# Attention and two MLP layers in one kernel: the first eight attention units in pairs, the second layer's raw weights fetched earlier, and operands of the sums split two ahead

## The chip, the cores and the metric

The kernel runs on one NeuronCore of a Trainium2 chip. Its time is device microseconds of one execution. TensorE (PE) multiplies matrices, VectorE (DVE) and ScalarE (ACT) work elementwise, and SyncE (SP) issues nearly all DMA. PE's weight loads have a track of their own (PEld).

## The reference

```python
# local and global attention: batch 4, 8 heads, 512 local + 32 global positions, head 64
s_g  = scale * q_g @ concat(k_g, k_l).T          # global rows see everything
out_g = softmax(s_g) @ concat(v_g, v_l)
s_ll = where(abs(pos_i - pos_j) <= 32, scale * q_l @ k_l.T, -1e9)
s_lg = scale * q_l @ k_g.T                       # local rows see a band and the global keys
out_l = softmax(concat(s_lg, s_ll)) @ concat(v_g, v_l)
x = concat(out_g, out_l)                         # 2176 tokens of 512
h = x @ w_in;  g = max(h, 0) + alpha * min(h, 0);  x = g @ w_out      # 512 -> 2048 -> 512
h = x @ w_in2; g = h * clip(h + 3, 0, 6) / 6;      out = g @ w_out2
```

All in float32 at full precision. The weights reach the chip as 64-bit words (float64).

## The kernel before, in words

Every product of the two layers is made of three: an operand is split into a rounded high part and the low rest, and high × high, low × high and high × low are summed. The high part is a copy on ACT, the low part a subtraction on DVE.

*Attention.* A unit is one batch, one half of the local positions and one pair of heads; there are 32. `local_units` (line 167) is a generator, and each `yield` ends a step. `load` fetches `q_t` and `k_t` (L173, L175), `load_v` the values `v_t` (L180). `scores` gives `s_ps` (L194); `softmax` reduces with the mask on DVE (L207), takes the exponential on ACT (L211) and the reciprocal `rs` on DVE; `transposes` makes `pt` (PE L222, copied by ACT L224); `values` gives `o_ps` (L235), scaled into `xo` by DVE (L241). The first eight units (`SINGLE`) run one at a time, the other 24 in pairs of two. `mask`, `ident` and `alpha` are loaded at the start (L73 to L75), `c1_sb` = 1 − alpha comes from the last of them (L76). `global_units` computes the 32 global rows of a pair of heads: `gq`, `gqz`, `gk`, `gv`, `gvg` are loaded (L302 to L310), scores `gs_ps`, transposes, and `go_ps` (L357): for each of the two heads four chunks of local values on 128 partitions and one of global values on 32.

*First layer.* `x_from_attention` transposes `xo` into `xt` (PE L386, ACT L372, DVE L373). A piece of weights is loaded as `raw` (L98) and turned into float32 on ACT (L113) and DVE (L117, L121, L123) as `z`, then split (ACT L129, DVE L130) into `wt`. There are five blocks of tokens (512, 512, 512, 256, 256). For each of 16 pieces j, `h_tile` gives `h_ps` (L401), `act` the activation `t`, `g` (ACT L411, DVE L413, ACT L419, DVE L420), and two steps later `y_tiles` adds into `y_ps` (L432). Block 0 runs as two lanes of 256 columns, the second four pieces behind; four products of zeros (L931) open its banks. The first layer's weights are converted during block 0. After each piece `attention_steps(STEPS[bi][s])` runs attention steps, and `SPLIT[bi]` steps of `second_weights` are spread over blocks 1 to 4: this generator fetches raws of the second layer, converts, splits, forms sums and differences, and stores them to DRAM (`wi` and `wo`, L506). Four buffers (`RAW`) are shared by raws and parts.

*Second layer.* It runs in two passes of 4 × 512 and 4 × 384 columns with seven products in place of eight. First the "in" products `k_ps` (L750) make tiles `far`; then the "sum" products `o_ps` (L830) take operands built from `far` by `operand` and split as `gh` (ACT L799) and `gl` (DVE L800). Weights stream from DRAM into eight buffers `ws` (L664 from `wi`, L669 from `wo`), issued by SP ahead of use. `inputs` prepares the input of the next pass meanwhile, one step per `next(more)`. The fifth block's rest follows (L897, L688).

The order of instructions on each engine is set by a scheduler when the program is built; what is wrapped in `here` keeps the order in which it is written. Each engine works its list in order, and an instruction waits for its inputs and for a free buffer (`bufs=`).

## Time and profile before

| | us |
|---|---|
| median of 3 runs | 855.52 (853.48 to 856.38) |
| the profiled execution | 853.92 |
| its span in the trace | 852.0 |
| PE busy | 827.0 (97%) |
| DVE busy | 592.8 (70%) |
| ACT busy | 415.2 (49%) |
| mean granted PE clock | 0.987 of full speed |

The span runs from the first to the last instruction; the execution's time is 1.9 us longer. A share of busy time is a mean over stages with different limits: attention with block 0 lies up to about 137 us, blocks 1 to 4 with the rest of attention and the second weights' preparation up to 497 us, and the second layer after it. The clock is given in shares of the full 2.4 GHz; the other level is 1.2 GHz.

### The profile page before, as it was taken

The page shows a single profiled execution, that of the slowest core. Times are in us where ns is not written, and L with a number is a line of the kernel's source. Part 1 is how long each engine was busy: PE and PEld are TensorE (multiplying, and loading weights), DVE is VectorE, ACT ScalarE, POOL GpSimd, SP SyncE. Part 2 cuts the span into 40 slices and gives each one's busy share as a digit, 9 for nine tenths or more (in the row PEclk, how much of TensorE's full clock was granted, in tenths as well). Part 3 has the DMA queues.
Part 4 walks back from the last instruction along what each step waited for, and adds up shares of the span by engine and source line. Part 5 has one row for each costly group of instructions (what it writes and reads, how often), then busy time and mean ns, then how long its engine had stood idle before and what let it go on. Part 6 is the DMA issues. An engine that isn't in the chain of part 4 may idle for free.

```text
span 852.0 us, 18369 instructions
## 1 busy us (share of the span) xinstructions
PE 827.0 (97%) x7232; PEld 745.6 (88%) x7232; DVE 592.8 (70%) x1321; ACT 415.2 (49%) x905; POOL 0.2 (0%) x4
## 2 busy tenths in 40 slices
PE   8898999999999999989999999999999998999997
PEld 5688999888878888878899998889999998999996
DVE  4898896576777777777778837879854787854221
ACT  5766665554556555455546523435532343443222
POOL 0000000000000000000000000000000000000000
PEclk7899999999999999999999999999999999999999
DMA  8994664476667765599776657668666887888882
GB/s 312 307 318 155 210 235 132 136 233 217 195 235 253 259 223 199 179 357 337 266 269 239 196 166 232 217 208 266 210 197 215 288 297 246 270 266 259 292 253 73
DMA packets 75780, 200.65 MB, mean 235 GB/s; under 512 B 7856, under 2 KB 24496, under 8 KB 74672
## 3 DMA queue, kind: packets, MB, share of 16 engines
q1 hardware_dynamic: 75600, 199.37, 70.4%
q8 instruction: 57, 0.93, 0.4%
q14 instruction: 27, 0.22, 0.1%
q10 hardware_dynamic: 96, 0.13, 0.1%
HBM read 157.00 MB, written 42.47 MB: 234 GB/s over the span
## 4 chain that ended last, share of the span: by engine, by line
PE 68%; DVE 12%; DMA 10%; ACT 7%; issue 2%; SPq 1%; ACTq 0%; DVEq 0%
PE o_ps L830 17%; PE k_ps L750 15%; PE y_ps L432 12%; PE h_ps L401 11%; DMA raw<-in_w 6%; PE h_ps L897 4%; PE o_ps L688 4%; DVE z L121 2%; DVE t L413 2%; ACT p L211 2%; PE s_ps L194 2%; DVE z L123 1%; ACT raw L113 1%; DMA ws<-wo 1%; DVE g L420 1%
## 5 line engine op out<-in xcount | busy, mean ns | idle before, releaser
L432 PE MATMUL y_ps<-g,wt 128*128 128x256 f32 (+2 forms) x1152 | 208.8, 332 | 5.8 <-ACT g L419 3.1
L401 PE MATMUL h_ps<-xt,wt 128*128 128x256 f32 (+2 forms) x1152 | 209.0, 331 | 1.8 <-ACT wt L129 0.8
L432 PEld LDWEIGHTS y_ps<-g,wt 128*128 128x128 f32 x1152 | 177.2, 191 | 23.1 <-ACT g L419 3.5
L401 PEld LDWEIGHTS h_ps<-xt,wt 128*128 128x128 f32 x1152 | 179.0, 191 | 20.5 <-DVE wt L130 1.5
L830 PE MATMUL o_ps<-ws,gh 128*128 128x256 f32 x784 | 141.1, 283 | 3.4 <-DMA ws<-wo 3.0
L750 PE MATMUL k_ps<-bt,ws 128*128 128x512 f32 (+1 forms) x672 | 136.8, 362 | 0.0
L750 PEld LDWEIGHTS k_ps<-bt,ws 128*128 128x128 f32 x672 | 120.8, 188 | 12.7
L830 PEld LDWEIGHTS o_ps<-ws,gh 128*128 128x128 f32 x784 | 121.2, 191 | 4.9 <-DMA ws<-wo 3.7
L830 PE MATMUL o_ps<-ws,gl 128*128 128x256 f32 x392 | 108.3, 283 | 0.0
L800 DVE TENSOR_TENSOR gl<-far,gh 128x1024 fp32r<-128x1024 f32 (+1 forms) x56 | 60.8, 1089 | 38.5 <-ACT gh L799 38.1
L799 ACT CAST gh<-far 128x1024 fp32r<-128x1024 f32 (+1 forms) x56 | 52.4, 942 | 63.3 <-PE o_ps L830 53.2
L830 PEld LDWEIGHTS o_ps<-ws,gl 128*128 128x128 f32 x392 | 73.6, 191 | 0.2
L413 DVE SCALAR_TENSOR_TENSOR t<-t,c_sb,h_ps 128x256 f32<-128x256 f32 (+2 forms) x96 | 55.2, 588 | 26.2 <-ACT t L411 26.0
L420 DVE TENSOR_TENSOR g<-t,g 128x512 fp32r<-128x512 f32 (+2 forms) x84 | 49.1, 586 | 23.1 <-ACT g L419 21.7
L419 ACT CAST g<-t 128x512 fp32r<-128x512 f32 (+2 forms) x84 | 45.0, 538 | 40.8 <-DVE t L413 36.4
L411 ACT ACTIVATE t<-h_ps 128x512 f32<-128x512 f32 (+2 forms) x84 | 42.8, 511 | 42.6 <-PE h_ps L401 39.3
L113 ACT ACTIVATE raw<-raw,quarter_sb 128x512 uint32<-128x512 uint32 x64 | 49.7, 777 | 26.4 <-DMA raw<-in_w 26.0
L211 ACT ACTIVATE p<-p,st 128x128 f32<-128x128 f32 x128 | 49.7, 390 | 16.6 <-DVE st L207 16.4
L735 ACT ACTIVATE t<-far,half_sb 128x512 f32<-128x512 f32 (+1 forms) x48 | 32.2, 670 | 47.4 <-DVE far L731 47.2
L121 DVE SCALAR_TENSOR_TENSOR z<-z,raw 128x512 uint32<-128x512 uint32 x64 | 43.9, 690 | 5.5 <-ACT raw L113 3.0
L123 DVE SCALAR_TENSOR_TENSOR z<-raw,z 128x512 uint32<-128x512 uint32 x64 | 43.7, 689 | 0.6
L897 PE MATMUL h_ps<-xt,ws 128*128 128x384 f32 x192 | 36.0, 336 | 0.0
(104 smaller groups left out, 868.5 us busy)
## 6 DMA issues: line engine op xcount, KB each, us to landing
ws<-wi SPq DMA_DIRECT2D x80, 512.0 KB, 4.9
ws<-wo SPq DMA_DIRECT2D x72, 512.0 KB, 4.3
raw<-in_w SPq DMA_DIRECT2D x64, 512.0 KB, 5.6
v_t<-in_vE SPq DMA_DIRECT2D x32, 512.0 KB, 6.6
wi<-raw SPq DMA_DIRECT2D x16, 512.0 KB, 2.9
wi<-parts SPq DMA_DIRECT2D x16, 512.0 KB, 4.6
wo<-raw SPq DMA_DIRECT2D x16, 512.0 KB, 3.2
wo<-parts SPq DMA_DIRECT2D x16, 512.0 KB, 6.1
```

The source lines that it names most:

```text
L113: here(nc.scalar.activation(low, low, AF.Relu, bias=quarter_sb, scale=0.9 * 2.0 ** -29))
L121: nc.vector.scalar_tensor_tensor(out=bits, in0=bits, scalar=3, in1=low, op0=ALU.logical_shift_left, op1=ALU.bitwise_or)
L211: nc.scalar.activation(p[:, n, :], p[:, n, :], AF.Exp, bias=st[:, 1, n:n + 1], scale=-1.0, accum_out=st[:, 2, n:n + 1])
L401: nc.tensor.matmul(ps[:, a:b], lhsT=wts[j][:, 0, wl, 128 * c:128 * c + 128], rhs=xt[c][:, xl, a:b], start=k == 0, stop=k == 3 * NC - 1)
L413: nc.vector.scalar_tensor_tensor(out=t[:, c:d], in0=t[:, c:d], scalar=c1_sb[:, j:j + 1], in1=ps[:, c:d], op0=ALU.mult, op1=ALU.add)
L420: nc.vector.tensor_tensor(out=g[:, 1, a:b], in0=t[:, a:b], in1=g[:, 0, a:b].bitcast(F32), op=ALU.subtract)
L432: nc.tensor.matmul(y[c][:, a:b], lhsT=wts[j][:, 1, wl, 128 * c:128 * c + 128], rhs=g[:, gl, a:b], start=first, stop=last)
L750: nc.tensor.matmul(bank, lhsT=wt[:, wl, at:at + 128], rhs=bt[x][:, c, xl, 0:w], start=first and k == 0, stop=k == 5, skip_group_check=True)
L799: nc.scalar.copy(hi, src)
L800: nc.vector.tensor_tensor(out=lo, in0=src, in1=hi.bitcast(F32), op=ALU.subtract)
L830: nc.tensor.matmul(bank, lhsT=part[:, jp, 128 * c:128 * c + 128], rhs=wo[:, jp, 256 * wl:256 * wl + 256], start=opens, stop=k == NP // 2 - ...
L897: nc.tensor.matmul(h, lhsT=wt[:, wl, 128 * c:128 * c + 128], rhs=xt[c][:, xl, 0:w], start=k == 0, stop=k == 3 * NC - 1)
```

## The change

- The first eight units run in pairs like the others. Scores of the first two pairs are computed before any transpose. SP loads the mask first, `ident` and `alpha` later, q and k of units 0 to 3 before any values; the values of these units go into free weight tiles, `vE` has two buffers instead of three. The early weight conversions come at other steps (`CONVERT`).
- `second_weights` fetches its next raw two steps earlier, and does none of its steps in the first two pieces of a block (`REST`).
- `global_units` multiplies the four local chunks of both heads first and then the global chunk of both.
- The four products of zeros that open the banks of block 0 are gone.
- In the stream, an "in" tile of which only one half is used is loaded by half.
- The operands of the sums come from a generator and are split two ahead, the first two during the last two rounds of the "in" products. One subtraction is done later (for "s3" instead of after "11"). The next pass's input preparation follows `MORE` and is kept in program order.

```diff
-SINGLE = 2 * HP
-SKEW = 1
-CONVERT = (5, 7, 9)
+CONVERT = (3, 4, 5)
+MORE = (1, 0, 8, 0, 0, 0, 8)
+REST = 2
...
     def load_constants():
-        nc.sync.dma_start(out=mask_sb, in_=mask)
         nc.sync.dma_start(out=ident_sb, in_=ident)
+        yield
         nc.sync.dma_start(out=alpha_sb, in_=alpha)
-        nc.vector.tensor_scalar(out=c1_sb, in0=alpha_sb, scalar1=-1.0, scalar2=1.0, op0=ALU.mult, op1=ALU.add)
+        yield
+        here(nc.vector.tensor_scalar(out=c1_sb, in0=alpha_sb, scalar1=-1.0, scalar2=1.0, op0=ALU.mult, op1=ALU.add))
...
         def load_v(u):
             b, hf, hp = units[u]
-            v_t[u] = att.tile([128, 8, 2, D], F32, tag="vE", name="v_t", bufs=3)
+            if u < FIRST_UNITS:
+                if u % 2 == 0:
+                    v2[u // 2] = wp.tile([128, 2, 8, 2, D], F32, tag="w", name="v_t", bufs=NJ)
+                v_t[u] = v2[u // 2][:, u % 2]
+            else:
+                v_t[u] = att.tile([128, 8, 2, D], F32, tag="vE", name="v_t", bufs=2)
...
         load(0)
-        load_constants()
+        nc.sync.dma_start(out=mask_sb, in_=mask)
         load(1)
+        constants = load_constants()
+        next(constants)
+        load(2)
+        load(3)
+        yield
         load_v(0)
-        load(2)
+        load_v(1)
+        next(constants)
         yield
-        load(3)
-        load_v(1)
+        pairs = [(u, u + 1) for u in range(0, n, 2)]
+        scores(*pairs[0])
         load_v(2)
+        load_v(3)
         yield
-        for lo, hi in ((0, FIRST_UNITS), (FIRST_UNITS, SINGLE)):
-            ...
-        pairs = [(u, u + 1) for u in range(SINGLE, n, 2)]
-        for j in range(len(pairs) + 1):
-            if j:
+        scores(*pairs[1])
+        next(constants, None)
+        load(4)
+        load(5)
+        yield
+        for u in pairs[0]:
+            transposes(u)
+        yield
+        values(*pairs[0])
+        load_v(4)
+        load_v(5)
+        for u in pairs[1]:
+            transposes(u)
+        yield
+        values(*pairs[1])
+        yield
+        for j in range(2, len(pairs) + 1):
+            if j > 2:
                 for u in pairs[j - 1]:
                     transposes(u)
                 yield
                 yield
             if j < len(pairs):
                 scores(*pairs[j])
-            if j:
+            if j > 2:
                 values(*pairs[j - 1])
             yield
             if j < len(pairs):
                 for u in pairs[j]:
-                    load_v(u)
+                    if j > 2:
+                        load_v(u)
                     if j + 1 < len(pairs):
                         load(u + 2)
             yield
...
+            os = [bank("go_ps") for _ in range(2)]
+            for cs in (range(4), range(4, 5)):
+                for h in range(2):
+                    pt, pt2 = pts[h]
+                    for c in cs:
+                        for b in range(B):
+                            nc.tensor.matmul(os[h][W * b:W * b + W, 0:D],
...
                 sums(z0, z1, k == 0)
                 store()
+                fetch()
                 yield
                 st = parts_tile()
                 hi(z, st)
                 yield
                 lo(z, st, dst[2 + k])
-                fetch()
                 yield
...
-            if key[0] == "in":
+            if key[0] == "in" and key[1] < len(twos) and key[3] == 1:
+                half = in_parts[key[2]][:, 1].rearrange("p (h c) -> p h c", h=2)[:, :, 256:512]
+                nc.sync.dma_start(out=t.bitcast(F32)[:, :, 256:512], in_=half)
+            elif key[0] == "in":
                 nc.sync.dma_start(out=flat, in_=in_parts[key[2]][:, key[3]])
...
+            def operands():
+                for what, _ in PRODUCTS:
+                    for pair in far:
+                        yield operand(what, pair)
+
+            coming, split = operands(), []
             for m in range(NP):
+                if m >= NP - 2:
+                    split.append(next(coming))
...
                 for k in range(NP // 2):
-                    hi, lo = operand(PRODUCTS[i][0], far[k])
+                    split.extend(islice(coming, 1))
+                    hi, lo = split.pop(0)
                     wo = take("sum", n, i, k)
...
-                    if i:
+                    for _ in range(MORE[i] * (k + 1) // (NP // 2) - MORE[i] * k // (NP // 2)):
                         next(more, None)
...
-            opened = still
-            for t in y:
-                nc.tensor.matmul(t, lhsT=still.to_broadcast([128, 128]), rhs=still.to_broadcast([128, 512]),
-                                 start=True, stop=False)
...
-            for _ in range(SPLIT[bi] * (s + 1) // (end + LAG) - SPLIT[bi] * s // (end + LAG)):
+            done = [SPLIT[bi] * max(x - REST, 0) // (end + LAG - REST) for x in (s, s + 1)]
+            for _ in range(done[1] - done[0]):
                 next(second, None)
```

How the program's order changes is seen at three places. The first is TensorE's list at the start, before and then after; `s_ps` are scores (sixteen rows to a unit), `pt_ps` transposes, `o_ps` values.

```order
L90 MATMUL warm_ps<-still 128x512 x8
L194 MATMUL s_ps<-k_t,q_t 32x128 x24
L222 MATMUL pt_ps<-ident_sb,p 128x128
L194 MATMUL s_ps<-k_t,q_t 32x128 x8
L222 MATMUL pt_ps<-ident_sb,p 128x128 x3
L194 MATMUL s_ps<-k_t,q_t 32x128 x8
```

```order
L92 MATMUL warm_ps<-still 128x512 x8
L201 MATMUL s_ps<-k_t,q_t 32x128 x64
L229 MATMUL pt_ps<-ident_sb,p 128x128 x9
L242 MATMUL o_ps<-v_t,pt 32x64 x16
L229 MATMUL pt_ps<-ident_sb,p 128x128 x5
L242 MATMUL o_ps<-v_t,pt 32x64 x16
```

The scores of four units now stand in one piece ahead of the first transpose; before, halves of units 1 and 2 stood between transposes.

The second is VectorE's list from the first `xo` on, before and then after; `z<-raw` begins a conversion of weights, `wt` ends it, `p,st<-s_ps` is a reduction of scores. Ahead of these rows stand twelve reductions before and sixteen after.

```order
L241 TENSOR_TENSOR xo<-o_ps,rs 128x256
L117 TENSOR_SCALAR z<-raw 128x512
L213 TENSOR_SCALAR st<-st 128x4
L215 RECIPROCAL rs<-st 128x4
L207 ISA p,st<-s_ps,mask_sb 128x128
...
L121 SCALAR_TENSOR_TENSOR z<-z,raw 128x512
L241 TENSOR_TENSOR xo<-o_ps,rs 128x256
L123 SCALAR_TENSOR_TENSOR z<-raw,z 128x512
```

```order
L248 TENSOR_TENSOR xo<-o_ps,rs 128x256 x2
L220 TENSOR_SCALAR st<-st 128x4
L222 RECIPROCAL rs<-st 128x4
L78 TENSOR_SCALAR c_sb<-alpha_sb 128x16
L119 TENSOR_SCALAR z<-raw 128x512 x2
L123 SCALAR_TENSOR_TENSOR z<-z,raw 128x512 x2
L388 TENSOR_TENSOR xt<-xt_ps,xt 128x256
L125 SCALAR_TENSOR_TENSOR z<-raw,z 128x512
```

The reductions of the fourth unit, which before stood inside the first conversion, have moved ahead of it, and the first two conversions run side by side.

The third is SP's list around the first global unit, before and then after; `raw<-in_w` are raw weights of the second layer here, `wo` its parts on the way to DRAM.

```order
L98 DMA raw<-in_w 128x512
L506 DMA wo<-parts 128x1024
L506 DMA wo<-raw 128x1024 x2
L302 DMA gq<-in_qgT 128x128
L304 DMA gqz<-in_qgT 64x128 x2
L306 DMA gk<-in_kN 128x2176
L308 DMA gv<-in_vN 128x2048
L310 DMA gvg<-in_vgN 32x512
L98 DMA raw<-in_w 128x512
```

```order
L100 DMA raw<-in_w 128x512
L521 DMA wo<-parts 128x1024
L100 DMA raw<-in_w 128x512
L521 DMA wo<-parts 128x1024
L521 DMA wo<-raw 128x1024
L314 DMA gq<-in_qgT 128x128
L316 DMA gqz<-in_qgT 64x128 x2
L318 DMA gk<-in_kN 128x2176
L320 DMA gv<-in_vN 128x2048
L322 DMA gvg<-in_vgN 32x512
L521 DMA wo<-raw 128x1024
L100 DMA raw<-in_w 128x512
```

Counted from the first raw of the second layer, the one straight behind `gvg` was the 53rd of 64. Now the 53rd is the second of the two ahead of `gq`, and the one behind `gvg` is the 54th.

## Rows read from the trace of the kernel before

**Rows 1.** The page's first part: busy us, share of the span, instructions.

```profile
PE 827.0 (97%) x7232; PEld 745.6 (88%) x7232; DVE 592.8 (70%) x1321; ACT 415.2 (49%) x905; POOL 0.2 (0%) x4
```

**Rows 2.** Stretches of the span: length, busy us by engine, PEclk, DMA share, GB/s.

```profile
0.00:16.00 16.00, 12.25 (x153) 7.76 (x159) 3.99 (x33) 7.41 (x28) 0.20 (x4) 0.74 0.85 283
16.00:34.00 18.00, 15.04 (x240) 11.51 (x239) 15.77 (x50) 12.46 (x35) 0.00 (x0) 0.76 1.00 341
34.00:137.00 103.00, 96.87 (x1206) 88.27 (x1196) 92.81 (x254) 69.48 (x172) 0.00 (x0) 1.00 0.66 224
...
360.00:380.00 20.00, 17.66 (x177) 15.58 (x176) 15.04 (x40) 10.50 (x26) 0.00 (x0) 0.91 1.01 354
...
560.00:600.00 40.00, 38.87 (x255) 35.19 (x254) 36.67 (x53) 20.58 (x33) 0.00 (x0) 1.00 0.80 258
```

**Rows 3.** Timeline of VectorE, 0 to 35 us: start, duration, what, [idle before it].

```profile
15.67 0.42 DVE L241 TENSOR_TENSOR xo<-o_ps,rs 128x256 f32<-128x256 f32 x1 [1.24 <-PE o_ps L235]
16.01 0.42 DVE L117 TENSOR_SCALAR z<-raw 128x512 f32<-128x512 f32 x1
...
17.14 0.29 DVE L207 CUSTOM_DVE_ANT_0 p<-s_ps,mask_sb 128x128 f32<-128x128 f32 x1 [0.41 <-PE s_ps L194]
...
17.99 0.69 DVE L121 SCALAR_TENSOR_TENSOR z<-z,raw 128x512 uint32<-128x512 uint32 x1
...
23.00 1.29 DVE L123 SCALAR_TENSOR_TENSOR z<-raw,z 128x512 uint32<-128x512 uint32 x2
...
33.77 0.87 DVE L413 SCALAR_TENSOR_TENSOR t<-t,c_sb,h_ps 128x256 f32<-128x256 f32 x2
```

**Rows 4.** Timeline of TensorE, 0 to 35 us.

```profile
8.02 1.08 PE L194 MATMUL s_ps<-k_t,q_t 64*32 64x128 f32 x16 [2.83 <-DMA k_t<-in_kE]
...
15.94 1.11 PE L194 MATMUL s_ps<-k_t,q_t 64*32 64x128 f32 x32
16.98 0.90 PE L222 MATMUL pt_ps<-ident_sb,p 128*128 128x128 f32 x3
```

**Rows 5.** Timeline of SP's DMA issues, 0 to 20 us.

```profile
3.06 0.43 SPq L173 DMA_DIRECT2D q_t<-in_qT  x1
3.53 0.43 SPq L175 DMA_DIRECT2D k_t<-in_kE  x1
```

**Rows 6.** Groups by line and shape on TensorE: busy us, mean ns.

```profile
L931 PE MATMUL y_ps<-still 128*128 128x512 f32 x4 | 2.2, 604 | 0.0
```

**Rows 7.** Timeline of all engines, 355 to 382 us.

```profile
359.25 0.63 SPq L98 DMA_DIRECT2D raw<-in_w  x1
...
368.09 0.43 DVE L117 TENSOR_SCALAR z<-raw 128x512 f32<-128x512 f32 x1 [1.79 <-DMA raw<-in_w]
...
371.60 0.41 ACT L419 CAST g<-t 128x256 fp32r<-128x256 f32 x1 [2.40 <-DVE z L123]
...
372.06 2.21 PE L432 MATMUL y_ps<-g,wt 128*128 128x256 f32 x12 [2.34 <-ACT g L419]
...
379.30 0.65 PE L357 MATMUL go_ps<-gv,gpt 128*32 128x64 f32 x32
...
379.89 0.31 PE L357 MATMUL go_ps<-gvg,gpt 32*32 32x64 f32 x8
```

**Rows 8.** The page's DMA issues: count, KB each, median us to landing.

```profile
ws<-wi SPq DMA_DIRECT2D x80, 512.0 KB, 4.9
ws<-wo SPq DMA_DIRECT2D x72, 512.0 KB, 4.3
raw<-in_w SPq DMA_DIRECT2D x64, 512.0 KB, 5.6
```

**Rows 9.** Waits by engine and line: us in total, times, longest.

```profile
PE o_ps L830 <- DMA ws<-wo: 3.0, 2, 2.3
...
PE o_ps L830 <- ACT gh L799: 0.5, 2, 0.3
...
DVE z L117 <- DMA raw<-in_w: 12.1, 9, 4.0
```

More of the change, by code (lines that the diff above doesn't have):

```diff
@@ L1 @@
 from contextlib import ExitStack
+from itertools import islice
 import numpy as np
@@ L168, in local_units @@
         units = [(b, hf, hp) for b in range(B) for hf in range(2) for hp in range(HP)]
-        q_t, k_t, v_t, p_t, rs_t, pt_t = {}, {}, {}, {}, {}, {}
+        q_t, k_t, v_t, p_t, rs_t, pt_t, v2 = {}, {}, {}, {}, {}, {}, {}
         def load(u):
@@ L200, in softmax @@
             b, hf, hp = units[u]
[L201 removed]
+            p = att.tile([128, 4, 128], F32, tag="p", name="p", bufs=FIRST_UNITS)
             st = att.tile([128, 4, 4], F32, tag="st", name="st", bufs=4)
@@ L421, in act, with y_tiles @@
         return g
-    def y_tiles(layer, y, g, wts, parts, opened=None):
+    def y_tiles(layer, y, g, wts, parts, lanes=False):
         for a, b, j in parts:
@@ L428, in y_tiles @@
             for (wl, gl), c in steps:
-                first = opened is None and j == 0 and (wl, gl) == (0, 0)
-                last = j == NJ - 1 and (wl, gl) == (0, 1) and (opened is None or b == 512)
+                first = a == 0 and j == 0 and (wl, gl) == (0, 0)
+                last = j == NJ - 1 and (wl, gl) == (0, 1) and (not lanes or b == 512)
                 if layer == 0:
                     nc.tensor.matmul(y[c][:, a:b], lhsT=wts[j][:, 1, wl, 128 * c:128 * c + 128], rhs=g[:, gl, a:b],
-                                     start=first, stop=last)
+                                     start=first, stop=last, skip_group_check=lanes)
                 else:
@@ L599, in columns, with inputs @@
         return sum(w for _, _, w in two[0])
-    def inputs(two, bt):
+    def inputs(two, bt, keep=lambda x: x):
         n = columns(two)
@@ L752, in product, with wide, total, parts_of @@
                         k += 1
+            def wide(tile_):
+                return tile_[:, :, 0:w]
+            def total(pool_):
+                return [pool_("o_ps") for _ in range((chunks + 1) // 2)]
+            def parts_of(src):
+                hi = wide(work.tile([128, 2, 512], F32R, tag="g", name="gh", bufs=LAG + 1))
+                lo = wide(later["xs"].tile([128, 2, 512], F32R, tag="gl", name="gl", bufs=3))
+                nc.scalar.copy(hi, src)
+                nc.vector.tensor_tensor(out=lo, in0=src, in1=hi.bitcast(F32), op=ALU.subtract)
+                return hi, lo
+            def operand(what, pair):
+                (a11, a12), (a21, a22) = ([pair[th][:, :, jh] for jh in range(2)] for th in range(2))
+                if what == "s1":
+                    add(a21, a21, a22)
+                elif what == "s2":
+                    add(a21, a21, a11, ALU.subtract)
+                elif what == "s4":
+                    add(a12, a12, a21, ALU.subtract)
+                elif what == "s3":
+                    add(a11, a22, a21, ALU.subtract)
+                return parts_of({"11": a11, "s1": a21, "12": a12, "s2": a21, "s4": a12, "s3": a11, "22": a22}[what])
+            def operands():
[3 more added lines that the diff above has]
+            coming, split = operands(), []
             for m in range(NP):
+                if m >= NP - 2:
+                    split.append(next(coming))
                 if m % 2 == 0:
@@ L787, in second_layer @@
             else:
[L788 to L819 removed]
+                more = inputs(twos[n + 1], bt_next, here)
             def summed(i, y, first=True):
                 for k in range(NP // 2):
[L823 removed]
+                    split.extend(islice(coming, 1))
+                    hi, lo = split.pop(0)
                     wo = take("sum", n, i, k)
```

73 lines of the change are left out of this document (11 added, 62 removed).

## The prediction

> **What bounds the kernel now.** I read the profile in this order: shares by engine, a table by stage, the list of waits, then the start and the 360–380 us stretch instruction by instruction. TensorE is busy 827.0 of 852.0 us [rows 1], so all that can be won without dropping matrix products is the 25.0 us in which it idles, and time in which it runs at the lower of its two clock levels, 1.2 instead of 2.4 GHz. The table by stage says where these lie [rows 2]: 3.75 us idle in 0–16, 2.96 in 16–34, 6.13 in 34–137, 2.34 in 360–380, 1.13 in 560–600 (stage length less PE's busy time), at mean clocks of 0.74, 0.76, 1.00, 0.91 and 1.00. The reader should see a second thing in the same rows: in 34–137 VectorE is busy 92.81 of 103 us. That stage, block 0, is paced by VectorE, which converts the first layer's weights there, and PE gets nothing to do before VectorE delivers. So the start matters through the time at which VectorE begins this work, not through PE's own idle time.
>
> The change touches five of these places. Each is priced against the profiled execution, 853.92 us; the median of the runs shown is 855.52, and I carry the sum over to it at the end.
>
> **1. The start.** VectorE's first weight conversion starts at 16.01, straight behind the first `xo` at 15.67, and the first `t` of the first layer, from which on block 0 runs, at 33.77 [rows 3]. Before that VectorE only reduces scores and waits for them. Scores of units 1 and 2 are computed in halves with transposes between; a half takes 1.08 us and can't start before unit 1's `k_t`, issued at 3.53, lands at 8.02, which is 4.49 us [rows 4, 5].
>
> After: SP issues mask, q1, k1 without ident and alpha between, two slots of 0.47 us earlier [rows 5], so k1 lands at 8.02 − 0.95 = 7.1, and k2, k3 (issued at 4.0 and 5.0 by the same slots, 4.5 us each) at 8.5 and 9.5. A whole unit's scores, undivided and at the low clock, took 1.11 us [rows 4]. So unit 1 is done at 8.2, unit 2 at 9.6, unit 3 at 10.6. Nine transposes stand next (three took 0.90 [rows 4], so 2.7: 13.3), then the values of unit 0 (1.1), five transposes (1.5), the values of unit 1 (1.1): 17.0, of which about half a microsecond overlaps, then two `xo` at 0.34 apart. The first conversion thus starts near 16.8, some 0.8 later than now. But all sixteen reductions of four units lie before it, where twelve do now. Between it and the first `t` the new order has four conversions of four operations, four `xt`, two `xo` and eight reductions. By [rows 3] these cost, less the 0.08 by which neighbours overlap (two of 0.69 take 1.29): 4 × (0.34 + 3 × 0.605) = 8.6, 4 × 0.335 = 1.3, 2 × 0.335 = 0.7, 8 × 0.215 = 1.7, together 12.3. First `t` at 16.8 + 12.3 = 29.1 instead of 33.77: 4.6 earlier. Before it, though, the old order had also done three of a fifth conversion's four operations (1.55) and the new one has done four reductions more (0.86), so 0.7 less work is behind it. **−3.9 us**, carried through block 0 because VectorE paces it. Bounds: if four units' scores run at the rate of the halves (2.1 us a unit), they end 3 us later and the gain is −1; if the clock stays high in the start and transposes and values take half, −6.5; and nothing, if raw weights or the loads ahead of them are late.
>
> The pairing itself, and the four opening products on zeros (604 ns each by the row, 2.2 us in all [rows 6]), lie where PE waits for VectorE. I count 0 for them; if that cover were gone, up to −2.2 for the zeros.
>
> **2. Fetch earlier, and the stall at 368.** SP issues the raw weights at 359.25, behind `gq`, `gk`, `gv`, `gvg`, over 2 MB; they land at 368.09, after 8.8 us, against a median of 5.6 [rows 7, 8]. VectorE's conversion waits 1.79 for them; its chain then holds the `t` behind which ScalarE's `g` starts at 371.60, and PE stands still 2.34 us until 372.06. The stage's mean clock of 0.91 over 17.66 busy us is another 1.6 us lost. In the new order on SP this raw, the 53rd of 64, goes out before `gq`. So the wait goes: 2.34 plus 1.0 of the 1.6 (a stretch at the low clock follows the stand): **−3.3 us**. Bounds: −3.9 and 0, the latter if `gk` then lands late and holds `gs` instead.
>
> The fetch also goes earlier in every other step of the split. That adds a wait on SP for a free raw buffer, and what is queued behind it there are loads of q, k, v and raws of the first layer. VectorE waits 12.1 us in all for raw weights, in nine places [rows 9]; the move may take some of these or add some. In 137–360 I see no PE idle time worth having, so 0 there.
>
> **3. Global units.** Per unit PE runs 32 products on 128 partitions (0.65 us) and 8 on 32 partitions (0.31), twice [rows 7]. Merged, one change of form is left of two. If the second group of eight costs what 8 of the 32 do (0.16), it saves 0.15 a unit: four units, **−0.5 us**. Bounds 0 and −1.2 (both groups).
>
> **4. The second layer.** PE waits 3.0 us in two places for the first `wo` weights of a pass and 0.5 for `gh` [rows 9]. Operands split two ahead take away the 0.5. Sixteen `in` loads are halved to 256 KB, so eight tiles' queue is shorter ahead of the first `wo`. That `wo` is issued only when a buffer comes free, though, and only some 12 products cover it, as now. I count 0.3 of the 3.0. **−0.8 us**; bounds −3.5 (both waits gone) and +3 (operand splits ahead of `far`, in program order, hold up the last `in` products: VectorE is 36.67 of 40 us busy in 560–600 [rows 2]). The moved subtraction is the same operation at another place: 0.
>
> The Trainium skill bears on the halved loads: its page "Perfetto Trace Analysis", section "DMA Optimizations", says "Small DMAs (< 2KB) have significant per-transfer overhead". The new pieces are 1 KB where they were 4 KB. In this trace the `wo` loads, in 2 KB pieces, take 4.3 us and the `wi` loads, in 4 KB pieces, 4.9 for the same 512 KB [rows 8], so no overhead shows down to 2 KB; no row here shows a 1 KB piece of this size. [...]
>
> **5. An allowance.** Queues, buffers (`vE` from three to two) and the order of the input split change in many places. One wait of the size of that in 560–600 (1.13) will come up somewhere: **+1.0 us**.
>
> Sum: −3.9 − 3.3 − 0.5 − 0.8 + 1.0 = −7.5, so 846.4 for a profiled execution, and 855.52 − 7.5 = **848.0** for the median, which I predict.
>
> **The rivals.**
> - *The start's gain is absorbed in block 0.* For it: VectorE waits for raw weights [rows 9], DMA is at 1.00 of its engines in 16–34 [rows 2], and values for four units are now loaded ahead of them. Against it: 0.66 in 34–137. Time: 855.52 − 3.3 − 0.5 − 0.8 + 1.0 = 851.9.
> - *The fetch doesn't do what it says:* `gk` or another load is late in place of the raws, since the same bytes go through the same queue. For it: DMA share 1.01 in 360–380 [rows 2]. Against: the raw that was late has then landed before. Time: 848.0 + 3.3 = 851.3.
> - *Both of them:* 855.2, no change.
> - *Slower: two value buffers instead of three.* SP issues a pair's `v_t` only after the values of the pair before; behind it on SP wait the raw weights of block 0. For raws VectorE waits 12.1 / 9 = 1.3 us each time over the whole program, 4.0 the longest [rows 9]. Six pairs lie in block 0. At 2 us of VectorE time each, 12 us are added: 855.52 − 7.5 + 12 = 860.0. It decides over slower from (7.5 + 2.6) / 6 = 1.7 us a pair. Against it: values are wanted late in a pair, and the next load is issued a pair ahead.
> - *More:* the start at its lower bound and both `wo` waits gone: 848.0 − 2.6 − 2.7 = 842.7.
>
> **Chances.** Forecast 0.61 (its own range 844.5 to 850.5), absorbed 0.16, fetch 0.07, both 0.06, slower 0.06, more 0.04. About 0.3%, 2.6 us, is what a measurement of this kernel can tell from no change: faster is below 852.9, slower above 858.1. The case of both is same; so is a third of absorbed and fetch, whose times lie close to 852.9. Faster 0.80, same 0.13, slower 0.07. For 8 in 10 the range reaches into the absorbed and fetch cases: 843.0 to 854.0.
>
> **What would show it.** In the profile after: first conversion on VectorE at 16–17.5, first `t` at 28–31, and PE bound (no idle time) some 4 us earlier than 137. The 53rd raw landed before `gk`, and no stand of PE for `g` of 2 us behind them, clock 0.97 or more in that stretch. The waits for `wo` still there, that for `gh` gone. The start is wrong if the first `t` comes early but block 0 ends no earlier; slower is right if VectorE's waits for raw weights grow from 12 towards 24 us in block 0, with SP held by `v_t`.

## The result and the profile after

The changed kernel takes 847.3 us (844.4 to 848.09, 5 runs) where the kernel before takes 853.48 beside it (852.63 to 856.38, 5 runs). The ratio is 0.9905, with an interval of 0.9881 to 0.993. The forecast was 848.0 and faster. Its sum was nearly met, −7.5 against −6.2 between these medians (−8.1 by the ratio), but by other terms than the ones that were added up, and that is luck. The profiled execution took 847.3, with a span of 845.5.

The page's line on TensorE, which answers to [rows 1], has to be read first:

```profile
PE 821.8 (97%) x7228; PEld 743.1 (88%) x7228; DVE 594.0 (70%) x1321; ACT 416.6 (49%) x905; POOL 0.2 (0%) x4
```

Idle time has hardly moved: 845.5 − 821.8 = 23.7 us, from 25.0. It is busy time that fell, by 5.2 us, with the same products less four. The table by stage answers to [rows 2] (length, busy us by engine, PEclk, DMA share, GB/s):

```profile
0.00:16.00 16.00, 12.07 (x207) 8.88 (x210) 4.63 (x41) 8.55 (x33) 0.20 (x4) 0.79 0.85 271
16.00:34.00 18.00, 13.85 (x201) 10.76 (x190) 14.67 (x49) 11.46 (x36) 0.00 (x0) 0.72 1.00 362
34.00:137.00 103.00, 97.53 (x1300) 90.33 (x1299) 95.92 (x267) 71.70 (x180) 0.00 (x0) 1.00 0.67 221
360.00:380.00 20.00, 16.00 (x216) 12.75 (x218) 14.70 (x41) 10.55 (x26) 0.00 (x0) 1.00 0.96 347
560.00:600.00 40.00, 40.00 (x285) 37.55 (x284) 31.96 (x37) 16.91 (x21) 0.00 (x0) 1.00 0.67 206
```

0–16 and 16–34 are no better (3.93 and 4.15 us idle on PE, 3.75 and 2.96 before). VectorE is busier in 34–137, 95.92 us from 92.81. The low clock is gone from 360–380, 1.00 from 0.91, and yet PE idles 4.00 us there, from 2.34. In 560–600 nothing is idle.

The stages shift against each other, so they are better cut by events: VectorE's first copy of `y_ps` at the end of block 0, its last one at the end of block 2, and the first product of the second layer. Before:

```profile
159.72 1.28 DVE L975 COPY ev<-y_ps 128x512 f32<-128x512 f32 x2
...
362.54 0.69 DVE L975 COPY ev<-y_ps 128x512 f32<-128x512 f32 x1 [0.34 <-PE y_ps L432]
...
497.53 1.78 PE L750 MATMUL k_ps<-bt,ws 128*128 128x512 f32 x7
```

After:

```profile
156.10 1.27 DVE L991 COPY ev<-y_ps 128x512 f32<-128x512 f32 x2
...
358.01 0.68 DVE L991 COPY ev<-y_ps 128x512 f32<-128x512 f32 x1
...
494.09 1.78 PE L768 MATMUL k_ps<-bt,ws 128*128 128x512 f32 x7
```

The differences of these starts and of the spans give the table on which all that follows rests. The kernels of the experiments stand in it too, each with its own profiled execution:

| kernel | first `t` | end of block 0 | blocks 1, 2 | block 2 to second layer | second layer | span |
|---|---|---|---|---|---|---|
| before | 33.77 | 159.72 | 202.82 | 134.99 | 354.47 | 852.0 |
| before, zeros out | 32.89 | 159.66 | 202.73 | 134.57 | 354.14 | 851.1 |
| before, pairs | 28.89 | 159.54 | 202.17 | 136.31 | 356.28 | 854.3 |
| changed | 32.08 | 156.10 | 201.91 | 136.08 | 351.41 | 845.5 |
| changed, again | 30.63 | 154.23 | 201.84 | 135.60 | 351.33 | 843.0 |
| old start | 33.36 | 157.74 | 201.85 | 135.44 | 350.87 | 845.9 |
| zeros back | 29.70 | 158.61 | 201.84 | 135.67 | 351.28 | 847.4 |
| fetch late | 30.23 | 157.57 | 201.80 | 137.27 | 350.76 | 847.4 |
| old sums | 30.52 | 154.83 | 201.90 | 135.38 | 355.59 | 847.7 |
| scores in order | 31.89 | 156.20 | 201.84 | 135.89 | 350.67 | 844.6 |
| full loads | 32.45 | 159.26 | 201.85 | 136.07 | 351.92 | 849.1 |
| fetch between | 30.13 | 153.65 | 202.65 | 134.33 | 350.97 | 841.6 |
| fetch between, again | 30.12 | 156.70 | 203.37 | 133.70 | 351.03 | 844.8 |
| values first | 32.50 | 157.88 | 202.77 | 133.75 | 350.30 | 844.7 |

From block 1 on the columns repeat within about 1 us where the new code of the stage is the same; with before's code the second layer lies between 354.14 and 356.28, the stretch ahead of it between 134.57 and 136.31. The end of block 0 repeats worst: with the same work it lies between 153.65 and 159.26. Part of that goes with the granted clock: from the first `t` to the end of block 0 the changed kernel's two traces took 124.0 and 123.6 us at 1.00, and the kernel with full loads, whose code is the same up to there, 126.8 at 0.97. So single profiles say much on the later stages and little on the start; for that the medians of the runs are needed.

The start, VectorE's timeline (start, duration, what, [idle before it]), answers to [rows 3]:

```profile
16.38 0.76 DVE L248 TENSOR_TENSOR xo<-o_ps,rs 128x256 f32<-128x256 f32 x2 [1.80 <-PE o_ps L242]
...
17.39 0.42 DVE L119 TENSOR_SCALAR z<-raw 128x512 f32<-128x512 f32 x1
18.41 0.43 DVE L119 TENSOR_SCALAR z<-raw 128x512 f32<-128x512 f32 x1 [0.59 <-DMA raw<-in_w]
...
22.21 0.42 DVE L388 TENSOR_TENSOR xt<-xt_ps,xt 128x256 fp32r<-128x256 f32 x1 [1.24 <-ACT xt L387]
...
32.08 0.48 DVE L428 SCALAR_TENSOR_TENSOR t<-t,c_sb,h_ps 128x256 f32<-128x256 f32 x1
```

The first conversion starts at 17.39 and the first `t` at 32.08, 1.7 us earlier than before where 4.6 were forecast. Waits of 2.0 us stand between, the longest for a raw (0.59) and for `xt` (1.24). TensorE's timeline shows where `xt` was late:

```profile
20.07 1.08 PE L242 MATMUL o_ps<-v_t,pt 128*32 128x64 f32 x32 [2.64 <-DMA v_t<-in_vE]
```

The values of unit 2, issued at 9.47 us behind a second raw, hold PE 2.64 us. In the second trace of this kernel (below) that wait is 0.3, and the first `t` comes at 30.63.

At the first global unit the wait for the raw is gone [rows 7], but the stand is not (all engines):

```profile
363.01 0.62 ACT L541 CAST parts<-z 128x512 fp32r<-128x512 f32 x1 [1.93 <-DMA wo<-raw]
...
366.35 1.69 PE L447 MATMUL y_ps<-g,wt 128*128 128x256 f32 x12 [1.35 <-ACT g L434]
...
369.23 1.70 PE L447 MATMUL y_ps<-g,wt 128*128 128x256 f32 x12 [1.19 <-ACT g L434]
...
372.94 0.66 PE L356 MATMUL gpt_ps<-ident_sb,gp 128*128 128x128 f32 x4 [1.46 <-ACT gp L344]
```

ScalarE now waits 1.93 us ahead of `parts` for a store to land, that is, for one of the four buffers that raws and parts share; `g` stands behind it, and PE waits twice for `g` and once for the exponential. These three waits, 4.00 us, are all of PE's idle time between block 2 and the second layer. Only the first of them changes with the wait for the buffer: in the second trace, where ScalarE waits 1.44 for it, they are 0.83, 1.22 and 1.46.

Over the whole program raw weights hold VectorE and ScalarE much less. ScalarE's waits for them, before:

```profile
ACT raw L113 <- DMA raw<-in_w: 26.0, 15, 4.9
```

After, with VectorE's, which were 12.1 [rows 9]:

```profile
ACT raw L115 <- DMA raw<-in_w: 5.6, 6, 2.8
...
DVE z L119 <- DMA raw<-in_w: 0.6, 1, 0.6
```

PE's waits by line, answering to [rows 9]: the first `wo` costs 1.1 us instead of 3.0, and `gh` is not in the list any more.

```profile
PE y_ps L447 <- ACT g L434: 2.8, 3, 1.4
...
PE o_ps L851 <- DMA ws<-wo: 1.1, 1, 1.1
```

### The profile page after: what moved, and what is told of

Same layout as the page of the kernel before. It is cut to its first block, busy times and chain, and to the rows that moved or that the text cites. A ratio compares the mean times of both kernels' runs of the same rounds, so it can differ in the third digit from the quotient of the medians.

```text
span 845.5 us, 18338 instructions
## 1 busy us (share of the span) xinstructions
PE 821.8 (97%) x7228; PEld 743.1 (88%) x7228; DVE 594.0 (70%) x1321; ACT 416.6 (49%) x905; POOL 0.2 (0%) x4
## 4 chain that ended last, share of the span: by engine, by line
PE 85%; DMA 6%; DVE 5%; ACT 2%; issue 1%; SPq 1%; ACTq 0%; DVEq 0%
PE h_ps L416 19%; PE y_ps L447 19%; PE o_ps L851 17%; PE k_ps L768 15%; PE h_ps L918 4%; PE o_ps L706 4%; DMA v_t<-in_vE 2%; DMA raw<-in_w 1%; PE o_ps L242 1%; PE s_ps L201 1%; PE pt_ps L229 1%; DVE z L123 1%; DMA wo<-raw 1%; PE xt_ps L401 1%; DVE z L125 1%; DVE wt L132 1%
## 5 line engine op out<-in xcount | busy, mean ns | idle before, releaser
L851 PE MATMUL o_ps<-ws,gl 128*128 128x256 f32 x392 | 106.6, 283 | 0.0
L218 ACT ACTIVATE p<-p,st 128x128 f32<-128x128 f32 x128 | 49.7, 390 | 12.6 <-DVE st L214 12.5
```

The lines of the kernel that those rows point to most:

```text
L218: nc.scalar.activation(p[:, n, :], p[:, n, :], AF.Exp, bias=st[:, 1, n:n + 1], scale=-1.0, accum_out=st[:, 2, n:n + 1])
L851: nc.tensor.matmul(bank, lhsT=part[:, jp, 128 * c:128 * c + 128], rhs=wo[:, jp, 256 * wl:256 * wl + 256], start=opens, stop=k == NP // 2 - ...
```

## The experiments

All kernels were timed in five rounds beside the kernel before (three for the full loads), on more than one chip, so they are compared by their ratios to it.

**Old start.** The changed kernel with before's first units:

```diff
-CONVERT = (3, 4, 5)
+CONVERT = (5, 7, 9)
-        for j in range(2, len(pairs) + 1):
+        for lo, hi in ((0, FIRST_UNITS), (FIRST_UNITS, SINGLE)):
...
```

> The changed kernel with the start of before: first eight units one at a time, scores of one unit before its transposes, constants loaded at once, three value buffers, conversions at the old steps; the zeros stay out and all other parts stay. Theory of the prediction (VectorE's first conversions set the start): about 3.9 us slower than the changed kernel's 847.3, so 851.2, with the first t of the first layer near 33.8 us and no other difference. Rival (single units cost in block 0, by TensorE's switching between scores and transposes and by VectorE's waits for what TensorE delivers late): also slower, by 2 to 4 us, but with the loss growing between the first t and the eighth, as VectorE's waits of 0.4 to 1.6 us between 40 and 73 us come back. Rival two (block 0 lost its waits to the missing zeros): under 1 us slower.

849.6 us (846.96 to 850.54), ratio to before 0.9912 (0.989 to 0.9934). The changed kernel's ratios are 0.9905 and, a second time, 0.9901 (below), so undoing the start costs 0.6 to 0.9 us by them, within intervals that overlap: not the 3.9. VectorE is busy 94.34 us in 34–137, between before's 92.81 and the changed kernel's 95.92. Block 0 ends at 157.74, inside the span of the kernels with pairs. The first `t` comes at 33.36, as the theory said, but the cost is of the size of rival two, under 1 us; that the missing zeros are its reason isn't shown by this run.

**Zeros back.** The changed kernel with the products on zeros:

```diff
+            opened = still
+            for t in y:
+                nc.tensor.matmul(t, lhsT=still.to_broadcast([128, 128]), rhs=still.to_broadcast([128, 512]),
+                                 start=True, stop=False)
```

> The changed kernel with the four opening products on zeros in block 0 again. Theory of the prediction: they lie where TensorE waits for VectorE, 0 us: 847.3. Rival: TensorE is late in block 0, VectorE's waits there follow it, and the products' 2.2 us show in full or in part: 848.5 to 849.5, with the start of the first t as now (32.1 us) or up to 2 us later.

848.47 us (846.18 to 850.38), ratio 0.9905 (0.9882 to 0.9928). By the ratios the zeros cost 0.0 to 0.3 us, with intervals that hold 0 and 2.2 alike. Block 0 ends at 158.61, but within what it varies by. Unclear by itself.

**Fetch late.** The changed kernel with the fetch as before and no rest:

```diff
-REST = 2
+REST = 0
-                fetch()
                 yield
                 st = parts_tile()
...
                 lo(z, st, dst[2 + k])
+                fetch()
```

> The changed kernel with the raw weights of the second layer fetched as before, after the low part, and with its steps spread over all pieces of a block again. Theory of the prediction: the stand of TensorE at the first global unit comes back, 3.3 us slower: 850.6. Rival (what the raw wait gave up, the wait of ScalarE for a free parts buffer behind a store took): 846.3 to 847.5, with one stand of TensorE of 2 us for g near 365 us instead of the two of 1.35 and 1.19.

846.55 us (843.52 to 849.45), ratio 0.988 (0.9854 to 0.9906): no slower, so the forecast's 3.3 us for this step are not there. The stand for `g` is back, as PE's waits below (total, times, longest) show, and another for `gk`, yet the stretch is longer by only 1.2 to 1.7 us (137.27). VectorE's and ScalarE's waits for raws are back as well, 12.5 and 26.4 us over the whole program. The run undoes the rest at the start of a block too, so it doesn't tell the two apart. PE's waits:

```profile
PE y_ps L447 <- ACT g L434: 2.6, 1, 2.6
PE gs_ps L329 <- DMA gk<-in_kN: 1.4, 1, 1.4
```

**Old sums.** The changed kernel with the second layer of before:

```diff
-                    split.extend(islice(coming, 1))
-                    hi, lo = split.pop(0)
+                    hi, lo = operand(PRODUCTS[i][0], far[k])
...
```

> The changed kernel with the second layer of before: operands of the sums split when used, all loads full, the next pass's input prepared one step per sum. Theory of the prediction: 0.8 us slower: 848.1. Rival from the trace of the changed kernel (the second layer there takes 351.4 us from its first product to the end, 354.5 before): 3.1 us slower, 850.4, with waits for gh near the second product of a pass and a wait for the first wo of some 2 us.

849.64 us (847.05 to 851.97), ratio 0.992 (0.9897 to 0.9943). The second layer takes 355.59 us, against 350.3 to 351.4 in the nine profiles that have all of the new one. By the stage the rival holds (4.2 us longer than in the changed kernel, 3.1 expected). By the ratios the run is 1.3 to 1.6 us slower, with intervals that hold both theories. PE's wait for the first `wo` is back:

```profile
PE o_ps L845 <- DMA ws<-wo: 3.2, 2, 2.0
```

**Full loads.** The changed kernel without the branch for the half tiles:

```diff
-            if key[0] == "in" and key[1] < len(twos) and key[3] == 1:
-                half = in_parts[key[2]][:, 1].rearrange("p (h c) -> p h c", h=2)[:, :, 256:512]
-                nc.sync.dma_start(out=t.bitcast(F32)[:, :, 256:512], in_=half)
-            elif key[0] == "in":
+            if key[0] == "in":
```

> The changed kernel with the sixteen halved loads of the second layer full again (512 KB for 256). With operands, loads and preparation all as before the second layer took 355.6 us, in the changed kernel 351.4. Theory of the prediction: the loads are worth 0.3 us, 351.7. Rival: they stand ahead of the first wo of a pass and decide when it lands; TensorE then waits about 2 us there again at each pass: 353 to 354. [...]

846.87 us (845.17 to 850.91), ratio 0.9918 (0.9895 to 0.994). The second layer takes 351.92, 0.5 more than in the changed kernel; the wait is 1.6 instead of 1.1:

```profile
PE o_ps L848 <- DMA ws<-wo: 1.6, 2, 0.8
```

By this one profile the halves are worth about 0.5 us (by the ratios 1.1 to 1.5, with intervals that overlap), and the operands and the order of the preparation the rest. A halved load lands little sooner than a full one of twice the bytes (the changed kernel: KB each, median us to landing; in its second trace 4.7 and 4.1):

```profile
ws<-wi SPq DMA_DIRECT2D x64, 512.0 KB, 4.8
ws<-wi SPq DMA_DIRECT2D x16, 256.0 KB, 4.5
```

**Scores in order.** The score products of the global units kept in the written order:

```diff
-                    nc.tensor.matmul(s[h][W * b:W * b + W, :], lhsT=q[64 * h:64 * h + 64, W * b:W * b + W],
-                                     rhs=k[64 * h:64 * h + 64, b, 0:SL], start=True, stop=True)
+                    here(nc.tensor.matmul(s[h][W * b:W * b + W, :], lhsT=q[64 * h:64 * h + 64, W * b:W * b + W],
+                                          rhs=k[64 * h:64 * h + 64, b, 0:SL], start=True, stop=True))
```

> The changed kernel with the score products of the global units kept in the order in which they are written, the two heads in turn; nothing is left out. In the changed kernel's trace three of the four units run them as two batches of eight, one head each, 1.06 us a batch, where sixteen in turn took 1.09 before. Theory: the batches, split by the scheduler once the heads' banks come free at other times, cost 3 times 0.8 to 1.0 us and ate what the fetch and the merged values won there: from the end of block 2 to the first product of the second layer 136.1 us fall to 133.5, and the whole by 2.5. Rival: TensorE waits in that stretch for the activations anyway, and the batches lie in that time: no change of the stretch beyond 0.5 us.

846.36 us (845.07 to 848.1), ratio 0.9914 (0.9883 to 0.9945), and the stretch is the same, 135.89. But the edit did not do what it was for. The scheduler still divides the group, now as one product and seven (two records each):

```profile
377.50 1.04 PE L329 MATMUL gs_ps<-gk,gq 64*32 64x512 f32 x2
378.47 1.10 PE L447 MATMUL y_ps<-g,wt 128*128 128x256 f32 x7
379.50 1.08 PE L329 MATMUL gs_ps<-gk,gq 64*32 64x512 f32 x14
```

Two records took 1.04 us and fourteen 1.08: a batch costs about 1 us whatever is in it. So the run tells nothing of an undivided group.

**Fetch between**, on the kernel above:

```diff
-                fetch()
                 yield
                 st = parts_tile()
                 hi(z, st)
+                fetch()
                 yield
```

> As the run with the global scores in order, and the next raw weights of the second layer fetched after the parts tile of the sum has been taken and not before it, one step later than in the changed kernel and one earlier than before. Theory: in the changed kernel the fetched raw takes the buffer that the parts tile needs, ScalarE then waits 1.9 us for a store to land, and g behind it holds TensorE twice (1.35 and 1.19 us); with the buffers taken in the old order these stands shrink to 1 us in all: 2.5 us on the same stretch beyond what the scores in order give, 131 us. Rival: the raw then lands later and VectorE's conversion waits in place of ScalarE's parts: the same stretch as without it, 133.5 us, give or take 0.5.

843.85 us (842.7 to 845.5), ratio 0.9885 (0.9857 to 0.9913). The stretch falls by 1.6 us to 134.33, where 2.5 were expected beyond the scores in order and 131 in all, and blocks 1 and 2 grow by 0.8. ScalarE's wait for the store is gone from the first global unit, and one for a raw of 3.5 us has come, much as the rival said, though it named VectorE and no gain:

```profile
ACT raw L115 <- DMA raw<-in_w: 3.5, 1, 3.5
```

**Fetch between, again.**

> The run with scores in order and the fetch behind the parts tile once more, on the chip and beside the runs of the kernel before with which the others of this call are compared. Theory: its median of 843.9 repeats within 1.5 us and lies 2 to 3 us under the changed kernel's. Rival: the first time was a good chip: 846.

846.61 us (843.58 to 849.88), ratio 0.989 (0.9853 to 0.9926). The two ratios lie 0.9 to 1.7 us under the changed kernel's, with intervals that overlap, so this version is not shown to beat it. Its trace shows the undivided group, though, in the third unit, beside a divided one in the second, of two and fourteen records again:

```profile
392.36 1.09 PE L329 MATMUL gs_ps<-gk,gq 64*32 64x512 f32 x16
```

Sixteen records in one piece took 1.09 us, and the two and fourteen 1.04 and 1.08.

**Changed, again.**

> The changed kernel unaltered, for a second profile on the chip of the other runs. Theory from the trace of the earlier runs: the start, whose loads share the DMA engines at full load, lands differently each time; the first t of the first layer comes at 30 to 32 us and the time moves with it, 845 to 848; from the end of block 0 on all stretches repeat within 0.5 us. Rival: the first t at 32.1 and block 0's length of 156.1 repeat.

844.86 us (843.33 to 848.39), ratio 0.9901 (0.9871 to 0.9931). The first `t` comes at 30.63, and block 0 ends 1.9 us earlier than in the first trace; all later columns repeat within 0.5.

**Zeros out of the kernel before**, the only edit:

```diff
-            for t in y:
-                nc.tensor.matmul(t, lhsT=still.to_broadcast([128, 128]), rhs=still.to_broadcast([128, 512]),
-                                 start=True, stop=False)
```

> The kernel before with one edit: the four opening products on zeros of block 0 are gone and the first product of each bank opens it. Theory of the prediction: they lie under VectorE's work, 0 us, ratio 1.000. Rival from putting them back (1.9 us slower at the medians, block 0 about 3 us longer): TensorE is late there, 2.2 us of its time come back, ratio 0.9975.

854.58 us (852.55 to 859.69), before 855.61, ratio 0.9991 (0.9968 to 1.0013). Neither theory is excluded; block 0 ends where it did.

**Pairs alone** in the kernel before: the new `local_units`, `load_constants` and `CONVERT`.

```diff
-CONVERT = (5, 7, 9)
+CONVERT = (3, 4, 5)
...
+        scores(*pairs[0])
...
+        scores(*pairs[1])
```

> The kernel before with one edit: the new start (first eight units in pairs, scores of four units in front, loads in the new order, two value buffers, new conversion steps). Theory of the prediction: the first t of the first layer comes about 4 us earlier and block 0 with it, 3.9 us, ratio 0.9954. Rival from the traces so far: the first t comes 2 to 3 us earlier, and block 0 ends 2 to 3 us earlier because VectorE's waits between 40 and 73 us go, ratio 0.997.

853.9 us (851.51 to 856.67), ratio 0.9975 (0.9955 to 0.9994): 2.1 us, the rival's size. The profile shows how the forecast's mechanism can fail: the first `t` comes 4.9 us earlier, at 28.89, and block 0 ends with before's, at 159.54. It is one execution, though, of 856.4 us where the median is 853.9, and before's profile is of 853.92 where the median beside this run is 855.61; the medians differ by 2 us, and so these two ends of block 0 don't stand for them.

After the first `t` PE waits for weights that VectorE and ScalarE have not finished:

```profile
39.34 1.22 PE L441 MATMUL y_ps<-g,wt 128*128 128x256 f32 x8 [1.37 <-DVE wt L129]
42.85 0.58 PE L410 MATMUL h_ps<-xt,wt 128*128 128x256 f32 x1 [2.29 <-ACT wt L128]
```

**Values first**, on the fetch-between kernel: values of units 2 and 3 straight behind those of 0 and 1.

```diff
         load_v(0)
         load_v(1)
+        load_v(2)
+        load_v(3)
         next(constants)
```

> As the run with scores in order and the fetch behind the parts tile, and in the start the values of units 2 and 3 are loaded straight behind those of units 0 and 1, ahead of alpha and the second raw weights. Theory: TensorE's wait of 1.0 to 2.6 us for v_t near 20 us goes, and the first t comes 1 to 2 us earlier, near 28.5; 1 to 1.5 us faster than that run. Rival: the same bytes through DMA engines at full load; the second raw lands later, VectorE's first two conversions wait for it, and the first t does not move: no difference.

847.19 us (844.65 to 848.65), ratio 0.989 (0.9859 to 0.992), no better than 846.61. The wait for `v_t` is 0.88 at its longest, 2.64 in the changed kernel; but in the two profiles of the kernel that this one is built on it was 0.8 and absent, so there was little to win. And `alpha`, now behind four value loads, holds VectorE 1.99 us, and the first conversion starts at 19.45:

```profile
19.36 0.17 DVE L78 TENSOR_SCALAR c_sb<-alpha_sb 128x16 f32<-128x16 f32 x1 [1.99 <-DMA alpha_sb<-in_alpha]
```

PE then waits 3.80 us for `xo`, which stands behind that on VectorE:

```profile
18.16 0.65 PE L242 MATMUL o_ps<-v_t,pt 128*32 128x64 f32 x32 [0.88 <-DMA v_t<-in_vE]
...
23.75 0.69 PE L401 MATMUL xt_ps<-ident_sb,xo 128*128 128x128 f32 x2 [3.80 <-DVE xo L248]
```

## Why the prediction was right, and where its steps failed

The time, the sign and the range held. The steps did so only in part.

**The start, −3.9.** The place was right in part, the mechanism not. Two steps failed. The first is the first `t`, "4.6 earlier": it came 1.7 and, in the second trace, 3.1 earlier. The work between the first conversion and it was sized nearly right, 12.3 us against 12.7, but the waits of 2.0 among it stood in the sum at nothing (only the lower bound names late loads), and the first conversion came at 17.39 and not at 16.8. The second step is "0.7 less work is behind it". How much VectorE had done at its first `t` is read from its busy time up to there, first before, then in the changed kernel and with pairs alone (the last fence also has the stretch after it):

```profile
0.00:33.77 33.77, 27.06 (x374) 19.07 (x380) 19.53 (x82) 19.64 (x61) 0.20 (x4) 0.75 0.93 313
```

```profile
0.00:32.08 32.08, 24.02 (x376) 17.71 (x377) 18.21 (x83) 18.09 (x59) 0.20 (x4) 0.73 0.93 318
```

```profile
0.00:28.89 28.89, 21.89 (x380) 16.02 (x380) 16.45 (x69) 16.58 (x50) 0.20 (x4) 0.82 0.93 328
34.00:50.00 16.00, 12.25 (x204) 10.03 (x207) 14.51 (x44) 11.45 (x33) 0.00 (x0) 0.74 0.71 241
```

VectorE was busy 19.53 us of 33.77, 18.21 of 32.08 and 16.45 of 28.89. Its idle time before the first `t` is 14.2, 13.9 and 12.4. So of the 4.9 us that pairs alone won for the first `t`, 3.1 are work put behind it and 1.8 are real. In the changed kernel 0.4 of 1.7 are real, and 1.6 of 3.1 in its second trace (17.98 us busy of 30.63), where the sum carried 3.9. In the stretch 34–50 of that execution of pairs alone PE then idles 3.75 us and runs at a mean clock of 0.74, and what was left is spent. The rival "the start's gain is absorbed in block 0" described this profile, with another reason; the median gain of 2.1 lies between it and the forecast.

**The pairing and the zeros, 0.** This was the other error, of the opposite sign. Block 0 did end about as much earlier as forecast, but not by the start. From the first `t` to the end of block 0, before and then after:

```profile
33.77:159.72 125.95, 119.82 (x1605) 110.47 (x1591) 105.69 (x312) 82.84 (x219) 0.00 (x0) 1.00 0.64 212
```

```profile
32.08:156.10 124.02, 118.53 (x1585) 110.93 (x1586) 106.23 (x310) 83.87 (x221) 0.00 (x0) 1.00 0.64 213
```

VectorE idles 20.3 us there before and 17.8 after. So of the 3.6 us in the first trace 0.4 come from its idle time ahead of the first `t`, 2.5 from its idle time behind it, and 0.8 from its busy time up to the end of block 0 (125.2 to 124.4). Products cost less when units run in pairs. By groups (busy us, mean ns, idle before) before:

```profile
L194 PE MATMUL s_ps<-k_t,q_t 64*32 64x128 f32 x1024 | 26.9, 288 | 3.2 <-DMA k_t<-in_kE 3.2
L222 PE MATMUL pt_ps<-ident_sb,p 128*128 128x128 f32 x128 | 22.1, 299 | 1.5 <-DVE st L207 0.9 <-ACT p L211 0.5
...
L317 PE MATMUL gs_ps<-gk,gq 64*32 64x512 f32 x64 | 5.0, 601 | 0.0
```

And after:

```profile
L201 PE MATMUL s_ps<-k_t,q_t 64*32 64x128 f32 x1024 | 23.9, 293 | 2.9 <-DMA k_t<-in_kE 2.9
L229 PE MATMUL pt_ps<-ident_sb,p 128*128 128x128 f32 x128 | 19.6, 291 | 1.6 <-ACT p L218 0.9 <-DVE st L214 0.5
...
L329 PE MATMUL gs_ps<-gk,gq 64*32 64x512 f32 x64 | 7.5, 601 | 0.0
```

Scores cost 3.0 us less, transposes 2.5 less, with the same counts; with the zeros' 2.2 that is 7.7 us of PE's time in and around block 0 (its whole busy time up to the end of block 0 fell by 4.3, from 146.9 to 142.6). My cover, "PE waits for VectorE", was not there all along: VectorE itself waits in block 0, in 34–137 of the kernel before 4.6 us for ScalarE's `wt`, 2.8 for its `t` and 0.9 for scores, and its idle time there fell from 10.2 to 7.1 us. The end of block 0 moved by 3.6 us in the first trace and 5.5 in the second, blocks 1 and 2 by 0.9 to 1.0. By the ratios, pairs alone give 2.1 us (0.5 to 3.8), and undoing them 0.6 to 0.9 within the intervals. That the cheaper products are the reason is not shown, and two runs speak against the most of it: pairs alone has them (44.6 us for scores and transposes, from 49.0) and wins 2.1, and the old start gives them back (49.4, from 43.5) and loses 0.6 to 0.9. What took the idle time out of block 0 stays open; no run separates the products from the new order of loads. The zeros' share stays open too: one run says 0.8 us, the other 0.0 to 0.3, with intervals on both sides of 0.

**The fetch, −3.3.** Wrong. The wait that was named went, and the clock with it, but the stretch from block 2 to the second layer is 136.08 and 135.60 us where it was 134.99 (134.57 and 136.31 in the two other kernels with before's code there). Against the fetch late it wins 1.2 to 1.7 us in that stretch and nothing that the medians show, although it takes 11.5 us of waits for raws from VectorE and 20.4 from ScalarE: nearly all of them were waits that PE didn't share. (The raw called the 53rd of 64 is counted from the program's first raw, those of the first layer included.) Two things took the place of the wait that went. One is a buffer, for which ScalarE waits 1.93 us ahead of `parts`. That the early raw takes it fits the run with the fetch between, where this wait is gone, but is not shown: with pairs alone, where the fetch is as before, ScalarE waits 2.61 us for such a store at the second global unit. The sum had asked what the earlier fetch does to SP's queue, not what it does to the ring of four. The other is in the rows of `gs_ps` above, 7.5 us from 5.0. In three of four units the scores of a global unit now run in two batches, each about 1 us:

```profile
376.09 0.43 PE L370 MATMUL go_ps<-gvg,gpt 32*32 32x64 f32 x16
...
378.06 1.06 PE L329 MATMUL gs_ps<-gk,gq 64*32 64x512 f32 x8
...
379.73 1.06 PE L329 MATMUL gs_ps<-gk,gq 64*32 64x512 f32 x8
```

Before, the third unit's were one batch:

```profile
397.73 1.09 PE L317 MATMUL gs_ps<-gk,gq 64*32 64x512 f32 x16
```

That is a change of the scheduler's order that the diff doesn't show; the forecast had looked at TensorE's new order at the start alone. The divided groups stand where PE waits for nothing, so nothing hides the second batch. Three batches more, at 1 us, are about what the fetch was to win. With the fetch late one group is divided and not three, and undoing the fetch made the kernel no slower. That an undivided group would win it back wasn't shown, since the run meant for it left the group divided.

**The global units, −0.5.** The mechanism was right and the saving larger: the two groups of `go_ps` took 5.2 and 2.5 us and now 4.4 and 1.7, 1.6 us less for four units; a pair of eights takes 0.43 [rows 7]. It goes down in the same stretch.

**The second layer, −0.8.** Under-sized. The second layer took 354.1 to 356.3 us in the three kernels with before's second layer and 355.59 with old sums, and 350.3 to 351.4 in the nine profiles with all of the new: about 4 us. I had counted 0.3 of the 3.0 us for the first `wo`; 1.9 went. The 0.5 for `gh` went as said. These 2.4 us are the fall of PE's idle time in the second layer in the first trace, from 8.5 to 6.1. The other 0.6 of that trace's 3.1 is busy time, 345.9 to 345.3. In pairs alone and old sums busy time is 347.2, and the granted clock is 0.91 in the 20 us that hold the second wait for `wo`; why it fell in these two profiles and not in before's is not shown. The Trainium skill ("Perfetto Trace Analysis", "DMA Optimizations") says that DMAs below 2 KB carry a significant overhead. The landing times bear it out in part: half the bytes in 1 KB pieces took 0.3 to 0.6 us less than all of them in 4 KB pieces, though the wait in the queue is in both. The run with full loads is 0.5 us longer in the second layer, so what the profiles show is a small gain.

**The allowance, +1.0.** Spent on the new waits, as the stand for `parts` shows, and too small for them.

Put together, by the first trace: −3.6 in block 0, −0.9 in blocks 1 and 2, +1.1 up to the second layer, −3.1 in it, −6.5 in all. The forecast had −3.9, 0, −3.8, −0.8 and +1.0. So it was luck that the total held: block 0 gained its 3.6 mostly in another way than the start's, and the second layer and blocks 1 and 2 made up for the fetch.

## What to carry to other kernels

When an event comes earlier, ask how much work its engine has done by then: an order that puts work behind the event makes it early for nothing. A wait is worth only what the slowest engine shares of it: some 32 us of VectorE's and ScalarE's waits for raw weights went here, and at most 1.7 us of the stage's length with them. A load moved forward can be paid for in the ring of buffers that it comes from, so count the ring's other users as well as the queue. And compare the new order of every engine at every stage on which a term rests, since a scheduler can divide a group of small products elsewhere, and what a group of small products costs may be set by the number of batches and not by their size.

## What the runs showed of the hardware

The global units' score products, on 64×32 tiles, cost by the batch: 2, 8, 14 and 16 records of 64×512 took 1.04, 1.06, 1.08 and 1.09 us at full clock. The same kernel's block 0 ended 1.9 us apart in two profiles of the changed kernel and 3.1 apart in the two of fetch between; the granted clock of the start fell differently in each (0.73 up to the first `t` in one trace of the changed kernel, 0.89 in the other).
